# Top-k attention followed by a feed-forward block: GpSimd works after the maximum, four vector operations move later in a step, and the last batch takes its last rows first

## The chip, the cores and the metric

The kernel runs on one core of a Trainium2 chip. The metric is the device time of one execution in microseconds (us), the median of several executions. The core has five engines that run side by side, each working through its own list of instructions in order: TensorE (PE in the profile; PEld is its weight load), VectorE (DVE), ScalarE (ACT), GpSimd (POOL) and SyncE (SP), which here only issues transfers. An instruction starts when those before it on its engine have gone and when the semaphores it waits for have been raised by other engines.

## The reference

The inputs are q, k and v with 8 batches, 8 heads, 576 rows and 64 columns, and the weights of a feed-forward block. Cut to what matters:

```python
scores = q @ k.T / 8                       # 576 x 576 for each batch and head
kth    = 32nd largest score of each row
attn   = softmax of the scores that are >= kth, others 0
x      = attn @ v, heads side by side      # 8 x 576 x 512
xn     = (x - mean(x)) / sqrt(var(x) + 1e-6) * g_ln
out    = x + relu(xn @ w_ch1) @ w_ch2      # 512 -> 2048 -> 512
```

Everything is float32. The costly parts are the search for the 32nd largest of 576 values in every row (VectorE), and the products (TensorE), above all the two of the feed-forward block.

## The kernel before

**Units.** The 576 rows of a batch are four tiles of 128 and a rest of 64. A job is one batch, one pair of heads (A and B, four pairs) and a list of row tiles. A unit is one row tile of a job: for a full tile 128 rows for each of the two heads, for the rest 64 rows of both heads together. There are 160 units, numbered 0 to 159, twenty for each batch. In batches 2 to 7 the first jobs take row tiles 0, 1 and the rest, and the next ones take 2 and 3. The row tiles of a job form a group: their softmaxed scores go into one tile `pt`, and `values` (L563, L570) multiplies the whole group by v at once.

**Steps.** The program is written as one loop over steps n (from L900 on), and the order of its calls is the order of the instructions on every engine. The unit numbers of one step differ: unit n has its 32 largest searched (`select`, VectorE); unit n+1 gets its scores (TensorE, L354; ScalarE copies them from PSUM, L335) and its halves (`halve`); unit n-1 is masked (ScalarE, L442); unit n-2, called `ex`, gets its exponentials (`weigh`, L452) and is turned; a group whose last unit is n-3 gets its `values` and is placed into x (`place`).

**The search.** From unit 8 on a row of 576 scores is split into two halves a and b. `halve` writes hi = max(a, b) on VectorE (L376) and lo = (a + b) - hi on GpSimd, in integer arithmetic on the bits, as two operations: the addition (L375) needs the scores alone, the subtraction (L377) needs hi. There is one buffer for lo and two for hi. `select` has four calls in a step: call 0 reads lo (L390) and call 1 to 3 take eight values at a time out of hi (L398) and strike them out (L385). `halve` for the next unit stands between call 1 and call 2.

**Turning.** Exponentials must be transposed before they meet v. TensorE does this against an identity matrix (L505, L538). For batches 2 to 7, head B of every unit but the last of its group is turned another way (`move`): VectorE transposes blocks (L482), a transfer writes the result to HBM and four more read it back into `pt` in its final order (L487, L489). The buffer of the scores of that unit holds the transposed data, and the unit four numbers on takes this buffer next. `turn_heads` (L304) transposes q and k of a job on VectorE; its loads for the following job are issued behind it.

**Reciprocals and statistics.** When a group is complete, VectorE takes the reciprocal of its sums (L932), and ScalarE multiplies by it as it copies the rows into x (L579). When a row tile of x is complete, `stats` has VectorE compute mean and variance (L629, L630) and GpSimd subtract the mean (L635, L638). TensorE may turn these rows (L667) from the next step on.

**The feed-forward work.** Two or three row tiles of x make a block. A block's TensorE work (turn the rows L667, hidden layer L680, output L697) goes into a list `todo`, at a step fixed beforehand (`gives`). `fill`, called eight times in a step, takes from that list as much as the planner (`slot`) allots to the step, so that each list is nearly empty when the next block is given. The rest rows of two batches make one row tile `r`, and the block that has it has three row tiles. In batch 7 it is the block of row tiles 0 and 1. What is left of the list after the last step is done at the end.

The parts that the change touches are `halve`, the three calls in the loop (`move`, `reciprocal`, `stats`), the list of jobs and the rule that makes blocks.

Of the kernel before, what the change touches and what calls it, by code (L numbers as in the profile page):

```python
# [10 lines left out]
ALU = mybir.AluOpType  # L11
FP32 = mybir.dt.float32
U32 = mybir.dt.uint32
I32 = mybir.dt.int32
# [7 lines left out]
J = 4  # L22
# [7 lines left out]
def kernel(  # L30
# [41 lines left out]
    nc = tc.nc  # L72
    P = nc.NUM_PARTITIONS
    B, H, S, D = q.shape
# [288 lines left out]
    def halve(u):  # L363

        nt = len(u.tiles)  # L370
        u.lo = lopool.tile([P, 2, HALF], FP32, tag="lo", name="lo")
        u.hi = hipool.tile([P, 2, HALF + TOP_K // 2], FP32, tag="hi", name="hi")
        a, b = u.sc[:, 0:nt, 0:HALF], u.sc[:, 0:nt, HALF:S]
        lo, hi = u.lo[:, 0:nt], u.hi[:, 0:nt, 0:HALF]
        nc.gpsimd.tensor_tensor(lo.bitcast(I32), a.bitcast(I32), b.bitcast(I32), ALU.add)  # L375
        nc.vector.tensor_tensor(hi, a, b, ALU.max)  # L376
        nc.gpsimd.tensor_tensor(  # L377
            lo.bitcast(I32), lo.bitcast(I32), hi.bitcast(I32), ALU.subtract
        )

    def select_halved(u, i):
        nt = range(len(u.tiles))
# [23 lines left out]
    def select(u, i):  # L406

        if u.halved:
            return select_halved(u, i)
        nt = range(len(u.tiles))  # L410
        if i == 0:
            u.cur = [u.sc[:, t] for t in nt]
            u.wk = {}
        m = small.tile([P, 2, 8], FP32, tag=f"m{i}", name=f"m{i}")
        for t in nt:
            nc.vector.max(m[:, t, :], u.cur[t])  # L416
        if i < TOP_K // 8 - 1:
            for t in nt:
                if i == 0:

                    o = (NF - 4 + 2 * t) * DM
                    u.wk[t] = w2[:].rearrange("p f n -> p (f n)")[:, o : o + S]
                nc.vector.match_replace(u.wk[t], m[:, t, :], u.cur[t], LOWEST)  # L423
                u.cur[t] = u.wk[t]
        if i == 0:
            u.top = m
        u.thr = m
# [50 lines left out]
    def move(u):  # L478

        i0 = place_of(u) // 32  # L480
        t = u.sc[:, 1, 0:JP]
        nc.vector.transpose(  # L482
            t.rearrange("p (j c n) -> p j c n", j=P // 32, c=J),
            u.e[:, 1, R:S].rearrange("p (c j k) -> p j c k", c=J, k=32),
        )
        hbm = hbmpool.tile([P, JP], FP32, tag="turned", name="turned")
        nc.sync.dma_start(hbm[:], t)  # L487
        for j in range(P // 32):
            nc.sync.dma_start(  # L489
                u.group.ptB[j * 32 : (j + 1) * 32, i0 : i0 + P // 32].rearrange(  # L490
                    "k i c n -> k i (c n)"
                ),
                hbm[:, j * P : (j + 1) * P].rearrange("(i k) x -> k i x", k=32),
            )
# [252 lines left out]
    for b in range(B):  # L747
        parts = [[0, 1], [2, 3], [J]]
        if b:
            parts = [[0, 1], [2, 3]]  # L750
            parts[b < 2].append(J)
        for qts in parts:
            jobs += [Job(b, hp, [qts]) for hp in range(NHP)]
    units = []
# [38 lines left out]
    for j in jobs:  # L793
        if j.hp == NHP - 1:
            b = j.b
            step = j.last + (3 if j.last < EARLY else 4)
            tiles = [(b, qt) for g in j.groups for qt in g.qts if qt < J]
            dsts = [[(out[b, t[1] * P : (t[1] + 1) * P, :], full)] for t in tiles]
            if J in j.groups[0].qts and b % 2:

                step += 1
                tiles.append(("r", b // 2))
                dsts.append(
                    [
                        (out[b - 1, JP:S, :], slice(0, R)),
                        (out[b, JP:S, :], slice(R, P)),
                    ]
                )
            if jobs.index(j) == NHP - 1:
                step -= 1  # L810
                j.groups[0].quick = True
            if tiles:
                add_block(step, tiles, dsts)
# [5 lines left out]
    def at(i):  # L819
        return units[i] if 0 <= i < N else None  # L820
# [59 lines left out]
    recips, rows_of = {}, {}  # L880
# [19 lines left out]
    for n in range(END):  # L900
        now[0] = n
        if n in gives:
            give(n)
        share[0] = slot(n)
        u, nxt, mk = at(n), at(n + 1), at(n - 1)
        ex, g = after(n)
        g = g if g and not g.quick else None
        late = at(n - 4)
        late = late if late and late.rest and late.job.b % 2 else None
        parts = turn(ex) if ex else []  # L910
        early = ex is not None and n - 1 < EARLY
        last = ex and ex is ex.group.units[-1]
        quick = ex.group if last and ex.group.quick else None

        moved = ex is not None and ex.moved
        order = (1, 0) if moved else (0, 1)
        sent, stores[:] = stores[:], []

        if ex and not early:
            weigh(ex, order[0])  # L920
        if nxt:
            scores(nxt)
        if g:
            values(g)
        if u:
            select(u, 0)
        if moved:
            move(ex)
        for store in sent:
            store()  # L930
        for den in recips.pop(n, []):
            nc.vector.reciprocal(den, den)  # L932
        if n == gives_first:
            for blk, i in rows_of.pop(n):
                blk.stats(i)
        if mk and mk.i >= CONVERTING:
            prepare(mk)
        if early:
            for t in range(2):
                mask(ex, t)  # L940
                weigh(ex, t)
        if not quick:
            weights(n, 0)
        fill()
        if ex and len(ex.tiles) > 1 and not early:
            weigh(ex, order[1])
        fill()
        if parts and not moved:
            parts[0]()
        if ex and ex.rest:  # L950
            keep_den(ex)
        if u:
            select(u, 1)
        if nxt and nxt.halved:
            halve(nxt)
        if n in turns:
            turn_heads(turns[n])
            later = fresh.index(turns[n]) + 1
            if later < len(fresh):
                load(fresh[later], nc.sync, nc.sync)  # L960
        for blk, i in rows_of.pop(n, []):
            blk.stats(i)
        if not quick:
            weights(n, 1)
        fill()
        if mk and not early:
            mask(mk, int(mk.moved))
        if g:
            place(g)
        if late:  # L970
            place_rest(late.job.b, late.job.hp)
        fill(1 if g or late else 0)
        fill()
        if moved:
            parts[0]()
        elif len(parts) > 2:
            parts[1]()
        if u:
            select(u, 2)
        for blk in gives.get(n - 2, []):  # L980
            blk.inverse()
        if last and ex.group.sums is not None:
            recips.setdefault(n + 1, []).append(ex.group.sums)
        last_rest = at(n - 3)
        if last_rest and last_rest.rest and last_rest.job.b % 2:
            hp = last_rest.job.hp
            den = dr[last_rest.job.b // 2][:, 2 * hp : 2 * hp + 2]
            recips.setdefault(n + 1, []).append(den)
        fill()
        if parts:  # L990
            parts[-1]()
        if mk and len(mk.tiles) > 1 and not early:
            mask(mk, 1 - int(mk.moved))
        fill()
        for x in (u if n < EARLY else None, mk if n > EARLY else None):
            if x and x is units[x.job.last]:
                load_values(x.job)
        if quick:

            values(quick)  # L1000
            for den in recips.pop(n + 1):
                nc.vector.reciprocal(den, den)
            place(quick)
            weights(n, 0)
            weights(n, 1)
        if u:
            select(u, 3)
            if u.i < CONVERTING:
                prepare(u)
        for x in (g, quick):  # L1010
            if x and x.job.hp == NHP - 1:
                for qt in x.qts:
                    if qt < J:
                        arrived(n, (x.job.b, qt), xs[x.job.b, qt])
        if late and late.job.hp == NHP - 1:
            r = late.job.b // 2
            arrived(n, ("r", r), rs[r])
        fill()
# [37 lines left out]
```

## Time and profile before

| what | value |
|---|---|
| device time, median of 3 | 1665.68 us (1665.18 to 1667.19) |
| span of the profiled execution | 1666.8 us |
| TensorE matmul busy | 1574.1 us, 94% |
| TensorE weight load busy | 955.1 us, 57% |
| VectorE busy | 1464.5 us, 88% |
| ScalarE busy | 1077.2 us, 65% |
| GpSimd busy | 664.0 us, 40% |
| chain of work that ended last | PE 71%, DVE 21%, no wait shown 4%, ACT 2% |

Busy time is the time in which an engine had an instruction under way; matmuls overlap, so the busy time of TensorE isn't the time that its work needs. The chain of work is followed back from the last instruction, at each step to what released it. A share over the whole span mixes stretches with different limits. VectorE stops about 130 us ahead of the end, when the last search is done; what follows is TensorE work on the last blocks. "Idle before" an instruction is how long its engine had nothing under way, with the instruction that ended it.

### The profile page before, as it was taken

How to read it: one execution, taken by the hardware profiler on the slowest of the kernel's cores; microseconds unless marked ns; L12 is line 12 of the kernel's file. 1: busy time of each engine (PE TensorE's matmuls, PEld its weight loads, DVE VectorE, ACT ScalarE, POOL GpSimd, SP SyncE). 2: the span in 40 equal slices, each digit the busy share in tenths (PEclk: the TensorE clock that was granted, in tenths of full speed). 3: DMA queues.
4: the chain of work that ended last, by engine and by line, in shares of the span. 5: the costliest groups of instructions: out<-in, count | busy, mean ns of one | idle time of the engine just before them, and what ended most of it. 6: DMA issues, size and time to landing. Idle time of an engine off the chain costs nothing.

```text
span 1666.8 us, 25284 instructions
## 1 busy us (share of the span) xinstructions
PE 1574.1 (94%) x7113; PEld 955.1 (57%) x7113; DVE 1464.5 (88%) x4476; ACT 1077.2 (65%) x2759; POOL 664.0 (40%) x879
## 2 busy tenths in 40 slices
PE   3568989989999999999999999999999999999998
PEld 1346556566555575755547575745547575755564
DVE  5998999999999999999999999899998999998000
ACT  5677967767666776767666675767666676665310
POOL 5567854343433434343343434343243433333010
PEclk9758999999999999999999999999999999999999
DMA  7423333001331133213231233112331132111000
GB/s 176 100 64 108 89 58 59 22 14 27 76 81 51 53 76 81 65 54 69 59 86 51 55 73 83 52 54 70 65 89 44 53 81 74 52 46 47 26 13 13
DMA packets 301203, 104.58 MB, mean 63 GB/s; under 512 B 246276, under 2 KB 283144, under 8 KB 301064
## 3 DMA queue, kind: packets, MB, share of 16 engines
q1 hardware_dynamic: 296328, 102.39, 24.4%
q10 hardware_dynamic: 4736, 0.59, 0.3%
q8 instruction: 57, 0.93, 0.2%
q14 instruction: 82, 0.67, 0.1%
HBM read 74.58 MB, written 28.31 MB: 62 GB/s over the span
## 4 chain that ended last, share of the span: by engine, by line
PE 71%; DVE 21%; issue 4%; ACT 2%; POOL 1%; DMA 1%; ACTq 0%; POOLq 0%; DVEq 0%; SPq 0%
PE hps L680 25%; PE ops L697 24%; PE scps L354 8%; PE av L563 6%; DVE m L398 5%; DVE hi L385 4%; PE tp L505 4%; DVE hi L390 2%; DVE m L416 2%; PE av L570 2%; DVE w L423 2%; DVE lo L385 1%; DVE hi L376 1%; DVE size L188 1%; PE tp L667 1%
## 5 line engine op out<-in xcount | busy, mean ns | idle before, releaser
L680 PE MATMUL hps<-xT,w 128*128 128x256 f32 (+1 forms) x2048 | 550.0, 411 | 2.7 <-ACT xT L672 2.3
L697 PE MATMUL ops<-w,h 128*128 128x512 f32 x1152 | 546.1, 599 | 0.0
L398 DVE MAX8 m<-hi 128x8 f32<-128x304 f32 x1088 | 460.7, 458 | 2.3
L680 PEld LDWEIGHTS hps<-xT,w 128*128 128x128 f32 x2048 | 372.1, 191 | 108.5 <-issue 17.3
L385 DVE MATCH_REPLACE8 hi<-m,hi 128x304 f32<-128x304 f32 x816 | 368.0, 456 | 0.0
L375 POOL TENSOR_TENSOR lo<-sc 128x576 int32<-128x576 int32 (+1 forms) x152 | 197.7, 1301 | 316.3 <-ACT sc L335 156.9
L697 PEld LDWEIGHTS ops<-w,h 128*128 128x128 f32 x1152 | 200.2, 191 | 169.9 <-issue 164.6
L377 POOL TENSOR_TENSOR lo<-lo,hi 128x576 int32<-128x576 int32 (+1 forms) x152 | 196.8, 1295 | 141.9 <-DVE hi L376 139.7
L354 PE MATMUL scps<-kT,qT 64*128 64x288 f32 (+3 forms) x1344 | 217.4, 433 | 32.4 <-DVE qT L304 20.9
L335 ACT COPY sc<-scps 128x288 f32<-128x288 f32 x576 | 199.2, 409 | 62.3 <-PE scps L354 51.0
L442 ACT ACTIVATE e<-sc,m 128x576 f32<-128x576 f32 x288 | 224.3, 779 | 9.7 <-DVE m L398 6.2
L452 ACT ACTIVATE e<-e,bias 128x576 f32<-128x576 f32 x288 | 224.6, 780 | 2.9 <-DVE bias L437 2.5
L390 DVE MAX8 hi<-lo 128x8 f32<-128x288 f32 x544 | 221.8, 443 | 2.6 <-POOL lo L377 1.5
L354 PEld LDWEIGHTS scps<-kT,qT 64*128 64x128 f32 (+1 forms) x1344 | 122.4, 181 | 146.6 <-issue 56.2
L505 PEld LDWEIGHTS tp<-ident,e 128*128 128x128 f32 x864 | 110.9, 147 | 115.9 <-ACT e L452 51.7
L505 PE MATMUL tp<-ident,e 128*128 128x128 f32 x864 | 138.1, 285 | 38.2 <-ACT e L452 37.9
L692 ACT ACTIVATE h<-hps 128x256 f32<-128x256 f32 (+1 forms) x256 | 105.9, 414 | 96.5 <-PE hps L680 93.8
L436 POOL TENSOR_TENSOR bias<-m,m 128x2 f32<-128x2 f32 (+1 forms) x143 | 27.8, 195 | 303.6 <-DVE m L398 303.6
L563 PE MATMUL av<-pt,vb 128*64 128x256 f32 (+2 forms) x1088 | 146.7, 413 | 0.0
L376 DVE TENSOR_TENSOR hi<-sc 128x576 f32<-128x576 f32 (+1 forms) x152 | 138.8, 913 | 5.5 <-ACT sc L335 5.5
L385 DVE MATCH_REPLACE8 lo<-hi,lo 128x288 f32<-128x288 f32 x272 | 118.2, 440 | 0.0
L517 ACT COPY pt<-tp 128x512 f32<-128x512 f32 x128 | 74.6, 583 | 62.1 <-PE tp L505 60.5
(79 smaller groups left out, 1295.0 us busy)
## 6 DMA issues: line engine op xcount, KB each, us to landing
turned<-sc SPq DMA_DIRECT2D x72, 256.0 KB, 2.0
pt<-turned SPq DMA_DIRECT2D x288, 64.0 KB, 2.0
vb<-in_v_dram SPq DMA_DIRECT2D x136, 128.0 KB, 2.5
raw<-in_moe_w_ch_dram SPq DMA_DIRECT2D x32, 512.0 KB, 4.0
kin<-in_k_dram SPq DMA_DIRECT2D x128, 72.0 KB, 2.5
qin<-in_q_dram SPq DMA_DIRECT2D x120, 72.0 KB, 2.5
out_dram<-o SPq DMA_DIRECT2D x32, 256.0 KB, 2.2
ends<-in_v_dram SPq DMA_DIRECT2D x136, 16.0 KB, 2.2
```

Of the source, the lines that this page charges most:

```text
L335: nc.scalar.copy(u.sc[:, t, s * HALF : (s + 1) * HALF], made[s][t][:, 0:HALF])
L354: nc.tensor.matmul(ps[i * R : i * R + ql, o : o + width], qT[r, q0 : q0 + ql], kT[r, k0 : k0 + width], start=True, stop=True,)
L375: nc.gpsimd.tensor_tensor(lo.bitcast(I32), a.bitcast(I32), b.bitcast(I32), ALU.add)
L385: nc.vector.match_replace(x[:, t], m[:, t, :], x[:, t], LOWEST)
L390: nc.vector.max(u.hi[:, t, o : o + 8], u.lo[:, t])
L398: nc.vector.max(m[:, t, :], u.hi[:, t])
L442: nc.scalar.activation(u.e[:, t], u.sc[:, t], AF.Prelu, bias=u.thr[:, t, 7:8], scale=-1.0, alpha=SLOPE)
L452: nc.scalar.activation(u.e[:, t], u.e[:, t], AF.Exp, bias=u.bias[:, t : t + 1], scale=-scale / SLOPE, accum_out=g.den[:, col : col + 1],)
L505: nc.tensor.transpose(ps[:, c * P : (c + 1) * P], u.e[:, t, c * P + t * R : (c + 1) * P + t * R], ident[:],)
L563: nc.tensor.matmul(av[h * D : (h + 1) * D, 0 : g.nq], vb[:, h * J + c, :], g.ptB[:, 0 : g.nq // 32, c, :] if h else g.pt[:, c, 0 : g.nq], ...
L680: nc.tensor.matmul(ps["h"][:, 0:N], w1[:, c, f * P : (f + 1) * P], xT[0][:, c, 0:N], start=(c == 0), stop=(c == NC - 1),)
L697: nc.tensor.matmul(ps[i][:], hT[f][:, i * P : (i + 1) * P], w2[:, f, :], start=(f == 0), stop=(f == NF - 1),)
```

## The change

Four edits go together.

1. In `halve`, GpSimd first subtracts hi from a and then adds b. The result is the same. Both operations now come after the maximum, and none of them can run at the same time as it.
2. `move` and the reciprocals go from right behind call 0 of `select` to behind `halve` and `turn_heads`. They are meant to find their inputs ready there.
3. `stats` goes from there to behind call 2 of `select`. (The first block's statistics stay where they are.)
4. Batch 7 takes its rest rows first, then row tiles 0 and 1, then 2 and 3. The tile `r` is then complete early, and it joins the block of row tiles 2 and 3 of batch 6, which waits for it. The blocks that are left for the end of the kernel have two row tiles each.

```diff
@@ halve
-        nc.gpsimd.tensor_tensor(lo.bitcast(I32), a.bitcast(I32), b.bitcast(I32), ALU.add)
         nc.vector.tensor_tensor(hi, a, b, ALU.max)
         nc.gpsimd.tensor_tensor(
-            lo.bitcast(I32), lo.bitcast(I32), hi.bitcast(I32), ALU.subtract
+            lo.bitcast(I32), a.bitcast(I32), hi.bitcast(I32), ALU.subtract
         )
+        nc.gpsimd.tensor_tensor(lo.bitcast(I32), lo.bitcast(I32), b.bitcast(I32), ALU.add)
@@ the list of jobs
             parts = [[0, 1], [2, 3]]
-            parts[b < 2].append(J)
+            if b < B - 1:
+                parts[b < 2].append(J)
+            else:
+                parts = [[J]] + parts
@@ the rule that makes blocks
+            if b == B - 2 and units[-1].job.b == B - 1 and J - 1 in j.groups[0].qts:
+                kept = (tiles, dsts)
+                continue
             if J in j.groups[0].qts and b % 2:
+                if not tiles:
+                    tiles, dsts = kept
                 step += 1
                 tiles.append(("r", b // 2))
@@ the loop over steps
         if u:
             select(u, 0)
-        if moved:
-            move(ex)
         for store in sent:
             store()
-        for den in recips.pop(n, []):
-            nc.vector.reciprocal(den, den)
...
             if later < len(fresh):
                 load(fresh[later], nc.sync, nc.sync)
-        for blk, i in rows_of.pop(n, []):
-            blk.stats(i)
+        for den in recips.pop(n, []):
+            nc.vector.reciprocal(den, den)
+        if moved:
+            move(ex)
...
         if u:
             select(u, 2)
+        for blk, i in rows_of.pop(n, []):
+            blk.stats(i)
```

## The prediction

> **What bounds the kernel now.** I read the page first (TensorE 94%, VectorE 88%), then the busy time in stretches, then what TensorE waited for in each, then single places in the timeline. The stretches are cut where TensorE last waited. Columns: stretch, its length, busy time of the engines with the count of instructions, granted TensorE clock, share of DMA, GB/s.
>
> ```profile
> 0.00:107.40 107.40, 51.19 (x191) 29.55 (x191) 89.42 (x191) 70.19 (x157) 56.70 (x63) 0.82 0.53 127
> 107.40:341.30 233.90, 206.99 (x1053) 134.15 (x1053) 227.21 (x696) 178.06 (x453) 142.91 (x154) 0.92 0.26 62
> 341.30:447.10 105.80, 103.62 (x505) 64.62 (x505) 103.75 (x329) 73.71 (x199) 41.72 (x64) 0.98 0.20 43
> 447.10:1503.40 1056.30, 1054.46 (x4814) 635.43 (x4815) 1009.93 (x3154) 706.22 (x1835) 402.08 (x571) 1.00 0.25 64
> 1503.40:1661.80 158.40, 157.85 (x554) 91.34 (x552) 34.23 (x111) 48.26 (x117) 19.34 (x28) 1.00 0.08 23
> ```
>
> Up to 341 us VectorE has no room (227.2 of 233.9) and TensorE has (207.0). From 447 us TensorE is busy for 1054.5 of 1056.3 us and then for 157.9 of 158.4, while VectorE idles 46 us in the long stretch. Is TensorE really full there, or do drawn-out matmuls hide gaps? The start-to-start distances of matmuls in the timeline say: 128 hidden matmuls of 256 columns take 27.7 us, 217 ns each; an output matmul of 512 comes every 0.43 us. With the distances of each kind, the work of 447 to 1503 us adds up to some 1026 us; the 30 us left over are pieces of about 0.2 us where one kind follows another, alike every time. The waits of TensorE after 341 us are these four alone:
>
> ```profile
> PE tp L667 <- POOL x L638: 4.8, 1, 4.8
> PE scps L354 <- ACT xT L672: 2.2, 1, 2.2
> PE hps L680 <- ACT xT L672: 1.5, 3, 1.1
> PE scps L354 <- ACT x L579: 0.9, 2, 0.6
> ```
>
> (waited for: us in total, times, longest). So the end is set by when TensorE gets to 341 us, plus its work, plus some 9 us of waits, most of them ahead of 450 us. A microsecond saved on VectorE behind that is worth nothing by itself.
>
> The collision that edit 1 removes, and the same maximum without it (start, length, engine):
>
> ```profile
> 922.37 1.41 POOL L375 TENSOR_TENSOR lo<-sc 128x576 int32<-128x576 int32 x1 [3.18 <-ACT sc L335]
> 922.47 1.92 DVE L376 TENSOR_TENSOR hi<-sc 128x576 f32<-128x576 f32 x1
> ...
> 904.55 0.74 DVE L376 TENSOR_TENSOR hi<-sc 128x576 f32<-128x576 f32 x1
> ```
>
> And the place where TensorE last waits long, for the statistics (edit 3):
>
> ```profile
> 338.66 0.69 DVE L629 BATCH_NORM_STATS2 st<-x 128x6 f32<-128x512 f32 x1
> ...
> 338.88 1.40 POOL L377 TENSOR_TENSOR lo<-lo,hi 128x576 int32<-128x576 int32 x1 [0.89 <-DVE hi L376]
> 340.25 0.19 POOL L635 TENSOR_SCALAR less<-mv 128x1 f32<-128x1 f32 x1
> 340.54 0.69 POOL L638 TENSOR_SCALAR x<-x,less 128x512 f32<-128x512 f32 x1
> ...
> 341.29 2.06 PE L667 MATMUL tp<-ident,x 128*128 128x128 f32 x8 [4.81 <-POOL x L638]
> ```
>
> **What the Trainium skill says.** "SBUF — State Buffer", section "Who interferes with whom": a vector operation with two inputs in SBUF and a GpSimd operation that reads SBUF exclude each other; the later one waits for the whole of the other. The trace agrees: the maximum began at 922.47, the addition ended at 923.78, the maximum 0.61 us after that. "TensorE: Matmul & The Clock Gate", section "What's actually happening": the clock is halved when TensorE has lately been little busy. The granted clock of 0.82, 0.92, 0.98 and 1.00 in the stretches agrees; behind the 2.2 us wait at 447 us the following `values` took 4.8 us in place of 2.95. "Perfetto Trace Analysis", section "Identifying the Most-Contended Engine", says that matmul busy time is no measure of TensorE's room; that is why I used start distances.
>
> **The change part by part.**
>
> *Edit 1, gain.* Of 120 maxima of full tiles (mean 1038 ns) the quickest take 0.74; the excess is 120 x 0.30 = 36 us. By time: 2.2 us of it ahead of 341, 2.5 between 341 and 447, the rest behind, where TensorE is full. So at most 4.7 of 36 us can count.
>
> *Edit 1, cost.* lo is ready later. Before: 0.14 us behind the maximum GpSimd takes 1.41. After: 0.14 + 1.41 + about 0.1 (the gap between dependent GpSimd operations, as 340.44 to 340.54) + 1.42 = 3.07 us. Between maximum and first use of lo (L390) VectorE has 3.97 us of work in a step of a full unit, but only 2.47 where a rest unit is searched and the next is full. There it waits 0.6 us. Up to 447 us that is four places (331, 357, 381, 406 us), 2.4 us, and one of them is ahead of 341. From batch 2 on, the moved transposition of edit 2 (0.62) fills the gap. Net lead of VectorE: 2.2 - 0.6 = 1.6 us at 341, and 4.7 - 2.4 = about 2.2 at 447 us.
>
> *Edit 3.* `stats` falls behind two maxima and two replacements, 1.65 us. At 341 us TensorE waits for just this: VectorE's lead of 1.6 and the delay of 1.65 cancel, TensorE goes on at the same time as before. The other row turns have either 7 us and more between subtraction and turn, or about 1 us (`r` at 453, 748, 1127 and 1507 us: 1.1, 1.3, 0.9, 1.3). The last three may cost 0 to 0.7 us each; mostly nothing, since the hidden layer behind waits for a ScalarE copy which stands behind the copies of the scores anyway.
>
> *At 447 us* TensorE waits 2.2 us for ScalarE, which waits for a threshold of VectorE. VectorE comes 2.2 us earlier, so that wait goes, and with it the 1.8 us at half clock: -4.0. Given back: the `pt` of the group used at 448 us now lands late (next item), about 1 us, and the turn of `r` at 453, about 0.5 to 1. I take -2.5 for the whole early part; bounds 0 (all given back) and -4.5.
>
> *Edit 2.* What it removes are waits of VectorE for exponentials (59.4 us, 19 times). Of these 38 us lie between 447 and 1503, where VectorE waits because TensorE is behind, and 21 behind 1503: nothing gained. What it adds: the block transposition comes 3.0 us later (call 1 and maximum) and 4.4 in the steps with `turn_heads`, where its transfer also queues on SyncE behind eight loads, 4.3 us of issue. From the end of the transposition of k: 4.35 + 2.0 (landing) + 1.8 + 2.0 = about 10 us until `pt` is there. `values` comes 12.5 to 14 us behind that point in all 22 such steps but the first (438.7 to 448.3). So nothing waits behind 450 us. The score copies four units on wait up to 2.4 us for the buffer; the next maximum comes 6 us later. A reciprocal comes 1.9 to 3.9 us later; ScalarE would wait up to 3.5 us for it around 280 us, where TensorE is ahead of VectorE by nearly 5 us anyhow, and under 2 us later. I take 0, with 0 to 5 us in the range.
>
> *Edit 4.* The blocks stay three, two and two row tiles, only in another order: hidden and output matmuls are the same in number. But the rest jobs are now groups of their own. Four more `values` of 64 columns cost 4 x 0.89; four shrink from 320 to 256 columns, 4 x (2.95 - 2.41); and row tile 1 is the last of its group, so its head B is turned by TensorE, 4 x 4 x 0.109. Sum 3.56 - 2.16 + 1.74 = +3.1 us of TensorE work where TensorE is full. That less work is left at the end gains nothing: TensorE is busy for 157.9 of the last 158.4 us, and it was so before. By the instruction list the steps of batch 7's rest units hold 36 us of TensorE work against 28 us of VectorE's, the next six 53 against 45, so TensorE doesn't run dry; 0 to 2 us for it.
>
> *Sum.* 1665.7 - 2.5 + 3.1 + 0.2 = 1666.5 us.
>
> **The rivals.**
>
> *A, the new waits reach TensorE: slower.* If in each of the 22 steps with `turn_heads` the later reciprocal and scores copy cost 0.3 us, and batch 7's rest units, with eight loads, two small transfers and four loads of v to a step, cost 2: 1666.5 + 6.6 + 2 = 1675. For it: ScalarE is in order, and 1 to 2 us of lateness at the old pace are in the trace. Against: VectorE gains 0.3 us a step and will run further ahead, which is where these come from.
>
> *B, VectorE sets the pace: clearly faster.* Chain 21% VectorE, busy shares 95% in the long stretch. If 20 of the 30 us of leftovers behind 447 us were its doing and went with the 31 us of VectorE time that the change saves there: 1666.5 - 20 = 1646. Against: the leftovers have the same length every time, whether VectorE waits or not.
>
> *C, the end gets shorter.* The block with three row tiles leaves the end: 28 us of TensorE work for one tile (13.8 hidden, 13.8 output). If it went into idle time: 1640. Against: there is none.
>
> *D, the early gain is whole.* TensorE keeps all 4.5 us, as the delayed reciprocals also shorten the wait at 341 and its half clock (2 us): 1665.7 - 6.5 + 3.1 = 1662.3.
>
> **How the numbers follow.** Forecast 0.52, A 0.20, B and C together 0.12, D 0.16. Within 0.2% is 1662.35 to 1669.0. The forecast case spreads by some 2 us and lies inside for most, 0.10 above and 0.04 below; D lies on the lower edge, about half below. Faster 0.12 + 0.08 + 0.04 = 0.24; slower 0.20 + 0.10 = 0.30; same 0.46. The range leaves out B and C and the upper part of A: 1660 to 1673.
>
> **What would show it.** No maximum over 0.8 us unless another GpSimd operation runs beside it; VectorE waiting 0.5 to 0.7 us for lo behind rest units; TensorE busy as fully from 450 us on; its wait at 341 about as long, that at 447 gone; 880 transpositions L505 in place of 864; VectorE ending its searches earlier relative to TensorE. I am wrong if TensorE has new waits behind 450 us (A), or if the long stretch has fewer leftovers between matmuls (B).

## The result, and the profile after

The changed kernel takes 1678.58 us (median, 1677.38 to 1679.97), the kernel before 1665.54 us on the same chip. The ratio is 1.0077, 95% interval 1.0059 to 1.0094: 0.8% slower. The prediction was 1666.5 us with a range of 1660 to 1673. The time lies outside the range; "slower" had been given a chance of 0.30.

The profiled executions span 1677.0 us after and 1666.8 us before, 10.2 us apart. Three views of the changed kernel show where they go. First the busy time in stretches, with the columns of the prediction (length, then TensorE, its weight load, VectorE, ScalarE and GpSimd with their instructions, clock, DMA share, GB/s):

```profile
107.40:341.30 233.90, 207.41 (x1052) 134.81 (x1052) 229.03 (x695) 177.96 (x453) 140.80 (x151) 0.93 0.25 62
...
447.10:1503.40 1056.30, 1049.98 (x4806) 630.07 (x4804) 964.32 (x3090) 698.66 (x1810) 389.87 (x560) 1.00 0.25 63
1503.40:1661.80 158.40, 158.40 (x634) 99.84 (x631) 53.81 (x176) 60.92 (x151) 29.15 (x40) 1.00 0.11 31
```

In the long stretch VectorE is busy 964.3 us in place of 1009.9. Edit 4 alone has 988.0 there, because it moves some of VectorE's work into the last stretch; the other 24 us fit what edit 1 was made for: the maximum of a full tile (128x576) takes 769 ns in the mean, before 1038. TensorE doesn't do more for it (1050.0 of 1056.3, before 1054.5). And up to 341 us, the only place where VectorE's time could count, VectorE has won nothing: from its first maximum of a split unit to the one ahead of the statistics at 341 us it takes 231.5 us (107.0 to 338.6), before 230.6 (107.4 to 338.0).

What TensorE waited for, first from 107 to 341 us, then from 341 us to the end (waited for: us in total, times, longest):

```profile
PE scps L354 <- ACT x L579: 5.7, 3, 4.2
...
PE scps L354 <- DVE den L967: 2.3, 1, 2.3
```

```profile
PE tp L667 <- POOL x L638: 4.6, 2, 4.3
PE av L563 <- DMA vb<-in_v_dram: 2.0, 1, 2.0
...
PE scps L354 <- ACT xT L672: 0.9, 1, 0.9
...
PE av L563 <- DMA dr<-den: 0.7, 1, 0.7
```

Against before, four lines are new or larger: the scores wait for ScalarE's copy into x (2.5 us before), the scores wait behind a reciprocal (`den`, none before), and `values` waits for a transfer twice (none before), at 451 us for v (`vb`) and at 670 us for what the profile names `dr`. More on that name below. The 2.2 us wait of the scores for `xT` at 447 us shrank to 0.9.

The third view compares the start of the scores in one step (they are those of the next unit) in the traces. As edit 4 alone (run below) does the same TensorE work as the whole change, the difference between these two is idle time, or time at a lower clock; all are given from the start of the span, in us. Edit 4 also changes how the planner spreads the work over the steps, so the row of the kernel before is to be compared at the first column and at the end.

| scores in step | 8 | 32 | 40 | 48 | 64 | 72 | 88 | 120 | end of span |
|---|---|---|---|---|---|---|---|---|---|
| kernel before | 109.9 | 335.3 | 409.2 | 478.5 | 628.1 | 702.1 | 853.3 | 1158.0 | 1666.8 |
| edit 4 alone | 108.2 | 333.3 | 407.3 | 476.4 | 625.9 | 700.0 | 850.3 | 1152.6 | 1668.1 |
| whole change | 110.1 | 337.8 | 410.6 | 482.6 | 632.2 | 708.0 | 859.4 | 1161.8 | 1677.0 |
| whole minus edit 4 alone | 1.9 | 4.5 | 3.3 | 6.2 | 6.3 | 8.0 | 9.1 | 9.2 | 8.9 |

The 1.9 us at step 8 stands in the row of the kernel before too (109.9 against 108.2). In the traces of all runs this start lies between 108.0 and 110.1 us, and at 108.8 in a run that differs from the whole change only later (v's loads early, below): it is how these executions started, no effect of the change. Then come +1.4 up to step 40, +2.9 between 40 and 48, +1.8 between 64 and 72, +1.1 between 72 and 88, and nothing behind. That is 7.0 us lost. With some 3.1 us of edit 4's work it makes the 10.2.

### The profile page after: what moved, and what is told of

Same layout as the page of the kernel before. It is cut to its first block, busy times and chain, and to the rows that moved or that the text cites. A ratio compares the mean times of both kernels' runs of the same rounds, so it can differ in the third digit from the quotient of the medians.

```text
span 1677.0 us, 25278 instructions
## 1 busy us (share of the span) xinstructions
PE 1581.9 (94%) x7201; PEld 963.2 (57%) x7201; DVE 1438.5 (86%) x4472; ACT 1080.5 (64%) x2767; POOL 659.8 (39%) x879
## 4 chain that ended last, share of the span: by engine, by line
PE 56%; issue 3%; ACT 1%; DVE 0%; DMA 0%; SPq 0%; POOL 0%; POOLq 0%; ACTq 0%
PE hps L680 19%; PE ops L697 19%; PE scps L354 6%; PE av L563 5%; PE tp L505 3%; PE av L570 2%; PE tp L667 1%; PE xo L602 0%; PE tp L538 0%; DMA turned<-sc 0%; POOL o L710 0%; ACT sc L335 0%; ACT xT L672 0%; ACT e L442 0%; PE tp L530 0%
## 5 line engine op out<-in xcount | busy, mean ns | idle before, releaser
L376 POOL TENSOR_TENSOR lo<-sc,hi 128x576 int32<-128x576 int32 (+1 forms) x152 | 197.2, 1297 | 560.4 <-DVE hi L375 327.8
L390 DVE MAX8 hi<-lo 128x8 f32<-128x288 f32 x544 | 222.2, 444 | 11.2 <-POOL lo L379 10.1
L379 POOL TENSOR_TENSOR lo<-lo,sc 128x576 int32<-128x576 int32 (+1 forms) x152 | 194.9, 1282 | 11.9
L375 DVE TENSOR_TENSOR hi<-sc 128x576 f32<-128x576 f32 (+1 forms) x152 | 106.6, 701 | 92.9 <-ACT sc L335 92.7
L563 PE MATMUL av<-pt,vb 128*64 128x256 f32 (+2 forms) x1152 | 151.5, 403 | 3.6 <-DMA vb<-in_v_dram 2.0
L563 PEld LDWEIGHTS av<-pt,vb 128*64 128x64 f32 x1152 | 78.6, 142 | 70.4 <-issue 28.7
```

Source lines behind the costliest of these rows:

```text
L376: nc.gpsimd.tensor_tensor(lo.bitcast(I32), a.bitcast(I32), hi.bitcast(I32), ALU.subtract)
L390: nc.vector.max(u.hi[:, t, o : o + 8], u.lo[:, t])
L563: nc.tensor.matmul(av[h * D : (h + 1) * D, 0 : g.nq], vb[:, h * J + c, :], g.ptB[:, 0 : g.nq // 32, c, :] if h else g.pt[:, c, 0 : g.nq], ...
```

## The experiments

Each single edit was run alone, then the parts that cost something were taken apart. Medians of "before" lie between 1665.5 and 1667.3 us by batch; the ratio is each time to the runs of before on the same chip, with its 95% interval.

**Edit 1 alone** (the first hunk of the diff).

> The kernel before with edit 1 alone (both GpSimd operations after the maximum). Theory (TensorE full from 450 us on; the 13 us come from edit 2's late transfers and from edit 4's extra work): the mean of the maximum of full tiles falls from 1038 to about 750 ns, but the time stays within 4 us of before, 1662 to 1668, since only what VectorE wins ahead of 450 us counts and the shift of the weights (L188) may now collide with GpSimd there. Rival B (VectorE sets the pace): 20 us faster, about 1646.

Measured: 1669.1 us, 1.0015 [1.0008, 1.0022], a little above the range of the theory. The maximum of full tiles falls to 779 ns. The wait for the statistics at 341 us is 6.26 us (4.81 before).

**Edit 2 alone**: `reciprocal` and `move` behind `turn_heads`.

> The kernel before with edit 2 alone (move and reciprocals behind the maximum and turn_heads). Theory: slower by 3 to 8 us (1669 to 1673), with waits of values (L563) for the turned transfers at about 450, 665 and 830 us or more often, since VectorE has not the lead that edit 1 gives. Rival (edit 2 costs nothing, the loss is all from edits 3 and 4): within 2 us of before.

Measured: 1674.63 us, 1.0042 [1.0030, 1.0055], above the range, and for another reason than expected: `values` waits, but not for the turned transfers. At 451 us it waits 2.0 us for `vb`, that is for v, and at 670 us 0.8 us for what the profile names `dr`. The scores wait 4.7 us at 213 us and 2.3 us at 281 us.

**Edit 3 alone**: `stats` behind call 2 of `select`.

> The kernel before with edit 3 alone (statistics behind call 2 of select). Theory: the turn of the rows at 341 us starts some 1.7 us later, and with it everything behind: 1666 to 1669. Rival (other waits take it up): within 1 us of before. A further rival: 5 us slower or more, if the rows of r at 453, 748, 1127 and 1507 us hold TensorE up too.

Measured: 1670.29 us, 1.0018 [1.0011, 1.0024], above the first range. The wait at 341 us is 5.84 us, 1.0 more than before; a new and larger one is that of the turn of `r` at 453 us, 2.1 us. Of the further rival's four places only this one shows.

**Edit 4 alone**: the order of batch 7's jobs.

> The kernel before with edit 4 alone (batch 7 takes its rest rows first). Theory: 3 us slower, 1668 to 1670, by TensorE's own extra work (16 transpositions and four more values), with TensorE as full as before behind 450 us. Rival C (a shorter end): faster by 10 us or more. Rival (batch 7's steps run dry): slower by more than 6 us, with waits of TensorE from 1330 us on.

Measured: 1669.81 us, 1.0020 [1.0014, 1.0027]. From the scores of step 8 to the end TensorE takes 3.1 us longer than in the kernel before, and behind 341 us no wait longer than 0.6 us is new.

The excesses of the four add up to 0.95%, the whole change has 0.77%. Edit 2, which the prediction put at nothing, is the largest.

**Edit 2 taken apart**: only `move` later, only the reciprocals later.

```diff
-        if moved:
-            move(ex)
...
             if later < len(fresh):
                 load(fresh[later], nc.sync, nc.sync)
+        if moved:
+            move(ex)
```

This is the first of the two; in the second the two lines of the reciprocals go the same way and `move` stays.

> The kernel before with only the move of edit 2 (block transposition and its transfers behind the maximum and turn_heads); reciprocals stay. Theory (the transfers queue on SyncE behind the eight loads and values waits for them): waits of TensorE at about 450 and 665 us, 3 to 5 us slower. Rival (the late reciprocals do all of edit 2's damage): within 1 us of before.

Measured: 1671.61 us, 1.0030 [1.0019, 1.0042]. The time is the theory's, the wait isn't quite: `values` waits 1.8 us at 449 us, for `vb`, not for `pt`.

> The kernel before with only the reciprocals of edit 2 later. Theory (ScalarE, in order, holds up the score copies in the stretch where VectorE sets the pace, 208 to 281 us, and the shift of the weights meets GpSimd): 1 to 3 us slower, all of it ahead of 345 us. Rival (edit 2's damage is all from the transfers): within 1 us of before.

Measured: 1667.35 us, 1.0005 [0.9998, 1.0011], the time of the rival. The scores wait 4.7 us at 214 us, yet the wait at 341 us shrinks from 4.8 to 2.7 us: TensorE comes later to a place where it waits anyway. A wait of 4.7 us at 214 us is worth at most 1.8 us at the end, by the upper end of the interval.

**The eight loads of k and q behind the move's transfers** (with edit 2), to try whether these loads are what delays `values`:

```diff
         if n in turns:
             turn_heads(turns[n])
-            later = fresh.index(turns[n]) + 1
-            if later < len(fresh):
-                load(fresh[later], nc.sync, nc.sync)
+        for den in recips.pop(n, []):
+            nc.vector.reciprocal(den, den)
+        if moved:
+            move(ex)
+        if n in turns:
+            later = fresh.index(turns[n]) + 1
+            if later < len(fresh):
+                load(fresh[later], nc.sync, nc.sync)
```

> Edit 2 as a whole, but the eight loads of the next heads are issued behind the move's transfers. Theory: the waits of values at 450 and 665 us go, and it is 3 us or more faster than edit 2 as it is (1674.6), about 1669 to 1671. Rival (it isn't the queue on SyncE but the later transposition itself): as slow as edit 2, 1673 to 1676.

Measured: 1678.01 us, 1.0066 [1.0054, 1.0079], slower than edit 2. That expectation fell. The wait that it meant to shorten grew:

```profile
PE av L563 <- DMA vb<-in_v_dram: 4.7, 3, 2.8
```

What grew names the cause. `values` doesn't wait for `pt` but for v, and v's four loads (two `vb`, two `ends`) are among the last things that a step gives to SyncE. Now the landing of the turned block stands ahead of all eight loads, and v comes behind everything. In the changed kernel SyncE's queue shows the same chain (start, length of the issue):

```profile
444.30 0.45 SPq L487 DMA_DIRECT2D turned<-sc  x1
447.12 1.91 SPq L489 DMA_DIRECT2D pt<-turned  x4
449.09 0.43 SPq L290 DMA_DIRECT2D vb<-in_v_dram  x1
...
450.12 0.59 SPq L290 DMA_DIRECT2D vb<-in_v_dram  x1
```

SyncE issues the write of the turned block at 444.30, then stands until it has landed, then issues four reads, and only at 449.09 the first load of v. From issue to landing this load takes 2.4 us in this trace; 449.09 + 2.4 = 451.5. And TensorE:

```profile
448.32 1.24 PE L354 MATMUL scps<-kT,qT 64*128 64x288 f32 x4 [0.87 <-ACT xT L672]
451.56 0.72 PE L563 MATMUL av<-pt,vb 128*64 128x320 f32 x2 [2.00 <-DMA vb<-in_v_dram]
```

The smaller waits at 670 and 833 us fit the same reading, though the profile names `dr` for the one and nothing for the other. The second load of `vb` is issued at 667.71 and at 829.83 us and lands 2.5 and 2.8 us later, at 670.2 and 832.6; the matmul of `values` that stood goes on at 670.61 and 832.82.

**v's loads early** (with edit 2): the test of that.

```diff
         for store in sent:
             store()
+        if n > EARLY and mk and mk is units[mk.job.last]:
+            load_values(mk.job)
...
-        for x in (u if n < EARLY else None, mk if n > EARLY else None):
-            if x and x is units[x.job.last]:
-                load_values(x.job)
+        if n < EARLY and u and u is units[u.job.last]:
+            load_values(u.job)
```

> Edit 2 (reciprocals and move later), with one thing more: v's loads of a job are issued near the start of the step, behind the stores, and so ahead of the turned transposition, its transfers and the eight loads of k and q, instead of at the step's end. Theory (v's loads hang at the end of SyncE's queue, behind the landing of the turned block): the waits of values at 451 and 670 us go, with the half clock behind the first, and the kernel comes out 2.5 to 4.5 us below edit 2 alone (1674.6), at about 1671; what stays over the kernel before is the later reciprocals and the late pt. Rival (values waits for pt, as the prediction named): the waits stay, now ended by the transfers into pt, time within 1 us of edit 2 alone.

Measured: 1669.97 us, 1.0020 [1.0012, 1.0028], 4.7 us below edit 2 alone. All waits of `values` for `vb` are gone, and the one at 670 us too. v is now on its way before the turned block is written:

```profile
435.61 0.43 SPq L290 DMA_DIRECT2D vb<-in_v_dram  x1
...
442.90 0.44 SPq L487 DMA_DIRECT2D turned<-sc  x1
445.88 1.74 SPq L489 DMA_DIRECT2D pt<-turned  x4
```

What is left is a wait of 0.7 us for `pt`. So v's place in SyncE's queue makes about half of edit 2's loss, or more (0.42% and 0.20% by the ratios, 8.0 and 3.0 us by the medians). The other half holds the reciprocals' 0.05% and that wait; it wasn't split further.

**Does VectorE set the pace late?** From unit 60 on (some 580 us) the first strike out of lo is left out, a part of the search:

```diff
-                if o == HALF:
+                if o == HALF and u.i < 60:
```

> The kernel before, leaving out from unit 60 on the first striking of eight values from lo, a part of the search: VectorE has some 0.9 us less to do in every step of 100, about 80 us in all, all of it behind 550 us. Theory (TensorE is full there and sets the end): time within 2 us of before. Rival B of the prediction (VectorE sets the pace in part): faster by 15 us or more.

Measured: 1666.79 us, 1.0001 [0.9993, 1.0009]. VectorE's busy time in the long stretch falls by 64 us (1009.9 to 946.1) and TensorE's stays at 1054.5:

```profile
447.10:1503.40 1056.30, 1054.46 (x4820) 634.10 (x4818) 946.06 (x2813) 706.35 (x1834) 411.32 (x573) 1.00 0.25 65
```

From unit 60 on VectorE's time is worth nothing: the interval leaves at most 1.5 us for 64. That settles rival B there; the next run does it from unit 48 on, some 470 us.

**Edit 1 from unit 48 on only.**

```diff
+        if u.i < 48:
+            nc.gpsimd.tensor_tensor(lo.bitcast(I32), a.bitcast(I32), b.bitcast(I32), ALU.add)
         nc.vector.tensor_tensor(hi, a, b, ALU.max)
...
```

> Edit 1 for the units from 48 on alone, where the prediction says that TensorE is full; the earlier units keep the addition beside the maximum. Theory (edit 1's loss of 0.15% arises in the early part alone, and its VectorE gain behind it counts for nothing): time within 1 us of before, maxima quick from 48 on. Rival (the later lo costs time in the long stretch too): 1.5 us or more slower.

Measured: 1667.07 us, 1.0000 [0.9994, 1.0007]. VectorE waits 11.2 us for lo, about as in the whole change (10.1), and that costs nothing that shows. So edit 1's 0.15% arises in the early part.

**The statistics earlier instead of later** (before, with the statistics of the first 47 steps right behind call 0 of `select`), and the same with edit 1:

```diff
-        if n == gives_first:
-            for blk, i in rows_of.pop(n):
+        if n == gives_first or n < 48:
+            for blk, i in rows_of.pop(n, []):
                 blk.stats(i)
```

> The kernel before with the statistics of steps up to 47 moved the other way, right behind call 0 of select, some 2.5 us earlier. Theory (TensorE's wait for the rows at 341 us, and the half clock behind it, pass to the end one for one): the wait falls from 4.8 to about 2.3 us and the time by 2 to 5 us, 1661 to 1665. Rival (what is won at 341 us is waited for again at 447 us): within 1 us of before.

Measured: 1664.55 us, 0.9986 [0.9979, 0.9992]: faster than before by 0.14%, and the fastest of all runs. The wait at 341 us is 1.9 us.

> Edit 1 whole, with the statistics of the units up to 47 right behind call 0 of select (the version that was 0.14% faster than before). Theory (edit 1's loss goes through the late statistics at 341 us, whose subtraction on GpSimd now queues behind two later operations of lo): with the statistics early, edit 1 costs under 1 us over the early statistics alone, time about 1665, not slower than before. Rival (edit 1's loss is the collisions with the weights' shift, which VectorE pays wherever the statistics stand): about 2.5 us over the early statistics alone, 1667.

Measured: 1665.54 us, 0.9996 [0.9988, 1.0004]. On top of the early statistics edit 1 costs 1.0 us by the medians and 1.7 by the ratios, whose intervals overlap a little. The time is the theory's and not slower than before, but the cost lies between theory (under 1) and rival (2.5). The wait at 341 us does what the theory says: with the statistics late, edit 1 lengthens it by 1.45 us, with the statistics early by 0.1 (1.9 to 2.0). How much of edit 1's time goes through it stays open.

**Do the causes add up to the whole?** Three versions of the whole change. First with v's loads early:

> The whole change, with v's loads of a job issued near the start of the step, behind the stores. Theory: of the changed kernel's 7 us of new idle time the parts at 451, 670 and 833 us and the half clock behind the first go (together some 5 us); the early 1.4 us and edit 4's 3.1 us of work stay, with some late pt; about 1673.5, ratio about 1.0045. Rival (in the whole change the waits sit on pt or elsewhere): within 1.5 us of the changed kernel.

Measured: 1673.33 us, 1.0038 [1.0025, 1.0050]: 5.3 us below the changed kernel, as expected. Against edit 4 alone its scores are 3.6 us late at step 40 and 4.3 at step 48 and at every one looked at up to step 120. So between 40 and 88 it loses 0.7 us, where the changed kernel lost 5.8. (Up to step 40 it loses 2.9 us, 1.5 more than the changed kernel in its one trace, so that part isn't known to better than that.) Then, besides, with the early order of lo's operations and of the reciprocals kept and the statistics behind call 0, up to step 47:

> The same, and up to step 47 the order of the lo operations and of the reciprocals is that of the kernel before, and the statistics stand right behind call 0 of select. Theory (what is lost is early idle time, v's loads and edit 4's work, and nothing else): only edit 4's 3.1 us are left, less the 1.5 to 2.5 us that the early statistics gained alone, so 1667 to 1668.5, ratio 1.000 to 1.001. Rival (the four edits together cost something in the long stretch that none shows alone): 1670 or more.

Measured: 1672.62 us, 1.0038 [1.0024, 1.0051]. That is the number of the rival, but the trace contradicts its reason: against edit 4 alone TensorE is 2.4 us earlier at step 40, 3.05 us later at step 48, and 3.05 us later at every step looked at from there to the last eight. So nothing is lost in the long stretch. The loss lies between these two steps, with waits at 448 and 433 us (the functions stand seven lines lower in this kernel, so that `values` is L570):

```profile
PE av L570 <- DMA pt<-turned: 2.3, 1, 2.3
PE tp L512 <- ACT e L459: 1.8, 1, 1.8
```

`move` was still late from step 42 on, TensorE came early, and so `values` at 448 us met the landing of `pt`. The last version therefore keeps the early places of `move` and of the reciprocals, too, up to step 59:

```diff
+        if n < 60:
+            for den in recips.pop(n, []):
+                nc.vector.reciprocal(den, den)
+            if moved:
+                move(ex)
...
-        if moved:
+        if moved and n >= 60:
             move(ex)
```

> The whole change with v's loads early, but edits 1 to 3 act from step 60 (edit 1: unit 60) on only; up to there the move, the reciprocals and the order of the lo operations are those of before, and all statistics stand behind call 0 of select. In whole_early_part_kept the move was late from step 42 on, and values waited 2.3 us at 448 us for pt's transfers, with a wait of 1.8 us at 433. Theory (edits 1 to 3 cost nothing behind 450 us once v's loads are early, and what is left is the early statistics' gain and edit 4's 3.1 us): 1666.5 to 1668.5, ratio 0.9995 to 1.001, no such wait at 448. Rival (edits cost something together in the long stretch): stays at about 1672.6.

Measured: 1667.41 us, 1.0005 [0.9996, 1.0013]. No wait of `values` is left. From step 60 on all four edits are in force, with v's loads early; up to there the statistics stand behind call 0. What remains is what two single runs add up to: 0.20% for edit 4, 0.14% won by the early statistics. Beyond what the interval leaves, some 1.4 us, nothing of the change's cost sits behind step 60 but v's loads and edit 4's work. This run puts the other orders of the steps 48 to 59 back together with `move`; that it was `move` which cost the 2.3 us rests on the wait for `pt`.

## Why the prediction was wrong, by its own steps

**TensorE is full from 447 us on: right.** Leaving out 64 us of VectorE's work behind 580 us changed nothing, and edit 1 from 470 us on alone changed nothing.

**"So at most 4.7 of 36 us can count", and the "net lead of VectorE: 2.2 - 0.6 = 1.6 us at 341": wrong; there was no such lead.** In the run of edit 1 alone VectorE comes from its first maximum of a split unit to the one ahead of the statistics in 230.3 us (106.0 to 336.4), before in 230.6: 0.3 us won. Runs whose early part is that of the kernel before scatter from 0.8 us less to 0.4 more, so even this isn't clear. The gain was set too high, and what was won was lost again on other operations. The groups of VectorE between 107 and 341 us, first before, then after (busy us, mean ns):

```profile
L376 DVE TENSOR_TENSOR hi<-sc 128x576 f32<-128x576 f32 (+1 forms) x25 | 19.5, 780 | 4.4 <-ACT sc L335 4.4
L188 DVE TENSOR_SCALAR size<-size 128x512 uint32<-128x512 uint32 x19 | 11.4, 638 | 0.0
L437 DVE TENSOR_SCALAR bias<-bias 128x2 f32<-128x2 f32 (+1 forms) x10 | 2.1, 206 | 0.3
```

```profile
L375 DVE TENSOR_TENSOR hi<-sc 128x576 f32<-128x576 f32 (+1 forms) x25 | 18.6, 745 | 2.2 <-ACT sc L335 2.2
L188 DVE TENSOR_SCALAR size<-size 128x512 uint32<-128x512 uint32 x19 | 12.5, 696 | 0.0
L437 DVE TENSOR_SCALAR bias<-bias 128x2 f32<-128x2 f32 (+1 forms) x10 | 4.7, 469 | 0.3
```

The maximum gained 0.9 us of the 2.2. At 117 us it stands beside GpSimd's work on the weights (L198) before and after alike (1.36 and 1.37 us), and at 241 us another operation of GpSimd (L710) took the place of the addition (1.56 and 1.58 us). The bias (L437), two elements a row, lost 2.6. It stands beside GpSimd's work on the weights (L194, L199), which the change doesn't move; VectorE comes to it at another moment. In edit 1 alone it loses 3.5 us (5.6 in all), and the operation ahead of it (L436) gains 2.7. The shift of the weights (L188) lost 1.1, but in edit 1 alone hardly anything (11.4 us, in one shift less), and with the later reciprocals alone 4.3 (15.7). One such place in the changed kernel, where a moved reciprocal stands between the maximum and the shifts:

```profile
169.30 0.75 DVE L375 TENSOR_TENSOR hi<-sc 128x576 f32<-128x576 f32 x1
...
169.97 0.17 DVE L967 RECIPROCAL den<-den 128x4 f32<-128x4 f32 x1
170.06 1.94 DVE L188 TENSOR_SCALAR size<-size 128x512 uint32<-128x512 uint32 x2
170.13 1.58 POOL L376 TENSOR_TENSOR lo<-sc,hi 128x576 int32<-128x576 int32 x1 [0.99 <-DVE den L967]
```

Two shifts take 1.94 us where two undisturbed ones take some 0.8: the second is over only when GpSimd's subtraction is. The Trainium skill, "SBUF — State Buffer", section "Who interferes with whom", lists beside the two-input operations that the prediction quoted the `tensor_scalar` in the modes that use both ports. L188 and L437 agree with it. The prediction read one clause of that list and asked only what was no longer beside the maximum, not what the other operations would now meet.

**A term that the prediction left out: GpSimd's own queue at 341 us.** The subtraction for the statistics (L635, L638) stands on GpSimd behind lo of the next unit. Before, one operation of lo was left behind the maximum, now there are two:

```profile
338.55 0.75 DVE L375 TENSOR_TENSOR hi<-sc 128x576 f32<-128x576 f32 x1
...
340.87 1.40 POOL L379 TENSOR_TENSOR lo<-lo,sc 128x576 int32<-128x576 int32 x1
...
341.58 0.18 DVE L630 BATCH_NORM_AGGREGATE mv<-st 128x2 f32<-128x6 f32 x1
...
342.23 0.19 POOL L635 TENSOR_SCALAR less<-mv 128x1 f32<-128x1 f32 x1
...
343.28 1.12 PE L667 MATMUL tp<-ident,x 128*128 128x128 f32 x4 [4.31 <-POOL x L638]
```

In the run of edit 1 alone VectorE has the mean ready at 337.9 us and GpSimd takes it up at 340.05, as the second operation of lo ends: 2.1 us later, before 0.7 us (339.6 to 340.25). That is the 1.4 us by which TensorE's wait grew.

**Edit 3, "VectorE's lead of 1.6 and the delay of 1.65 cancel": wrong, for both reasons.** There was no lead, and both numbers are VectorE's, while in the changed kernel GpSimd's second operation of lo ended last (342.2 us, the mean 341.8). In the single runs the wait at 341 us grew by 1.5 us (edit 1) and by 1.0 us (edit 3); in the whole change it is 4.3, since TensorE came there later itself. The run with the statistics earlier shows the size of this place from the other side: 0.14% gained. Edit 3 alone has its larger new wait elsewhere, 2.1 us for `r` at 453 us, where the prediction had 0.5 to 1; in the whole change the wait for v at 451 us comes first and nothing of it is left.

**Edit 2, a reciprocal later costs nothing "around 280 us, where TensorE is ahead of VectorE": right in the time, wrong in the place.** ScalarE did wait, more than the 3.5 us named:

```profile
213.42 0.93 ACT L579 ACTIVATE x<-xo,den 128x64 f32<-128x64 f32 x4 [4.13 <-DVE den L967]
...
281.50 0.93 ACT L579 ACTIVATE x<-xo,den 128x64 f32<-128x64 f32 x4 [4.96 <-DVE den L967]
```

TensorE waited behind it for 4.2 and 2.3 us, and won most of that back at 341 us: alone the later reciprocals cost 0.05%, with an interval that holds zero.

**Edit 2, "So nothing waits behind 450 us": wrong, and the largest error.** The prediction followed the transposition's own transfers to `pt` and found them needed 12.5 us or more behind, where they take about 10. On SyncE it counted what stands ahead of them, the eight loads, and left out what stands behind them: v's loads. These cost 1.8 + 1.1 = 2.9 us at 670 and 833 us, and at 451 us a wait of 2.0 us with a lower clock behind it. The clock in stretches (length, TensorE busy, granted clock, DMA share, GB/s), first before, then after:

```profile
448.00:452.00 4.00, 4.00 (x17) 0.57 0.03 2
```

```profile
452.00:456.00 4.00, 3.65 (x15) 0.57 0.05 7
```

So the half clock that the prediction counted as won was only moved. In the trace of the whole change with v's loads early the granted clock is 1.00 from 444 to 460 us.

**"At 447 us ... that wait goes ... -4.0", given back 1.5 to 2: the wait went, but more was given back.** It fell from 2.2 to 0.9 us, and the wait for v took its place a few us later. Between step 40 and 48 the change lost 2.9 us instead of gaining. With v early, `pt` is next in line there (0.9 us in the whole change, 2.3 us where TensorE came earlier), which is the landing that the prediction had in its sum at 1 us.

**Edit 4, +3.1 us: right**, 3.1 us by the traces and 3.2 by the medians, and TensorE doesn't run dry in batch 7.

**The sum.** The "-2.5 for the whole early part" measured 1.4 + 2.9 = +4.3; edit 2's nothing behind 450 us measured +2.9; edit 4 was right. That is 9.7 of the 12.1 us between the forecast and the median. The two medians are 13.0 us apart, the two profiled spans 10.2, and the difference is in the execution of before that was profiled: it took 1668.59 us, 3.0 above its median, while that of after, 1678.76 us, stands at its own. The rest of the 12.1 can't be read from these two traces. Rival A had the right kind, and the sign that was named for it, new waits of TensorE behind 450 us, is what came. Its time, 1675, was near, but not its place: its many small waits in all 22 steps with `turn_heads` didn't show; three did, at 451, 670 and 833 us, behind v's loads, which it named for batch 7's rest units alone.

## What to carry to other kernels

An operation moved away from a collision can meet another, and it holds up what stands behind it on its own engine: list what runs on both engines in the slot it moves to and what is queued behind it, in every phase of the kernel, not only in the one that the collision was seen in. When an issue on an in-order DMA queue is made later, or waits for a landing, look at everything that the queue holds behind it and at who needs that first; here it was one of the last loads of a step. A phase in which the bound engine is full forgives waits elsewhere, so look for the cost in the few places where it isn't.

## What was not expected of the hardware

An operation on 128x2 elements (L437) takes 0.17 us in the median and up to 1.20 us beside GpSimd. In the changed kernel three of its ten, at 138, 164 and 187 us, take 1.13 to 1.20 us and end within 0.03 us of the operation of GpSimd beside them: here the collision costs as much as is left of the other operation, though one's own is small. And a wait of TensorE costs more or less than itself: behind the 2.0 us wait at 451 us the following 4 us ran at a granted clock of 0.57, while the 4.7 us wait at 214 us, ahead of a place where TensorE waits anyway, hardly reached the end.
